# A written-out order for the first mixture, new pools for the second, and its first factors moved ahead

## The chip, the cores and the metric

The kernel runs on one core of a Trainium2 chip. Its time is the device time of one execution, in microseconds. A core has TensorE (PE in the profile; PEld are its weight loads), VectorE (DVE), ScalarE (ACT), GpSimd (POOL) and SyncE (SP, here only a queue for transfers). Each engine works through its own queue in order and waits there for results of the others.

## The reference, cut to what matters

```python
x = attention(q, k, v, centroids)       # 2 x 8 heads, 768 rows, width 64; (1536, 512) afterwards
h = x @ w_in                            # first mixture: (1536, 512) @ (512, 2048)
g = h * (1.0 / (1.0 + np.exp(-h)))
x = g @ w_out                           # (1536, 2048) @ (2048, 512)
P = sinkhorn(x @ w_gate)                # second mixture: eight experts, all of them for every row
for e in range(8):
    out += P[:, e:e+1] * (np.maximum(x @ w1[e], 0.0) @ w2[e])     # 512 -> 1024 -> 512
```

`w_in` and `w_out` come as 64-bit floats, the other inputs as 32-bit floats.

## The kernel before, in words

Products are made of a high and a low part: each operand is split into a rounded high part on ScalarE and the rest on VectorE or GpSimd, and three matmuls (high by high, high by low, low by high) stand for one.

The attention comes first and has an order written out by hand. The part of interest follows it.

*First mixture.* The 2048 hidden columns are cut into four slices. For each slice there are two passes of twelve tiles, so 8 passes and 96 tiles, numbered T = 0 to 95 here. A pass has three chunks of 512 rows, a chunk four tiles of 128 columns; a tile is twelve matmuls into one of eight PSUM banks (pool `mp`). In the first pass of a slice (L565 with `xh`, `xl`) a tile's result goes through a sigmoid on ScalarE (L582), a product on VectorE (L583, which is the last to read the bank), a high part on ScalarE (L584) and a low part on GpSimd (L585). In the second pass (L565 with `gh`, `gl`) a tile's result is added to `acc1`: a copy on ScalarE in the first slice (L598), a VectorE addition in the others (L600). These are called totals below.

The 64-bit weights are narrowed in steps: per pass one block n (n = 1 to 7 in these passes, block 0 during the attention), in four pieces of 128 x 512. A piece takes, on ScalarE, `wb` (L104), `w0` (L106) and the high part `wh` (L128); on VectorE `w1` (L107), `w2` (L109), `w3` (L110), `w4` (L112) and `wp1` (L114); on GpSimd `wp0` (L113) and the low part `wp2` (L129). Block n is narrowed while pass n - 1 runs. In this part the kernel leaves the order on each engine to the scheduler: the loop calls the four pieces of a block after the first four tiles of a pass, and the scheduler interleaves them.

*Second mixture.* Each of 16 slices (expert, half of its hidden width) has two layers of seven products (a scheme with seven block products in place of eight). A product of layer a is 24 matmuls (L815), one of layer b 36. The order of its instructions on four engines is written out by hand. Before a product, the weight's factor is split (`factor`: L713 on ScalarE, L638 on VectorE; tiles `wfh`, `wfl`), in slice 0 also x's factor (`x_factor`: L726, L638; `xfh`, `xfl`), some after sums of blocks of `acc1` (`x_sum`, L635). The blocks of `acc1` are halves of its rows by halves of its columns. In layer a the order of products is p = 1, 2, 6, 5, 7, 3, 4; products 1, 6, 7 and 4 add up in one set of three banks, and after product 1 ScalarE must copy this set (L852) before product 6 goes on with it. Between the last four stand the matmuls of the gate (L758, L765). The pools of this mixture are laid out one behind the other over the memory that the first mixture leaves, and a tile waits until whatever lies under it has been read for the last time.

Of the kernel before, what the change touches and what calls it, by code (L numbers as in the profile page):

```python
# [8 lines left out]
F32 = mybir.dt.float32  # L9
F32R = mybir.dt.float32r  # L10
# [3 lines left out]
ALU = mybir.AluOpType  # L14
# [24 lines left out]
def attention_moe_kernel(ctx, tc, kq, vp, cent, w_in, w_out, w_gate, w1, w2, out):  # L39
# [7 lines left out]
    def r(t):  # L47
        return t.bitcast(F32)
# [68 lines left out]
    def wsplit_steps(n, k, pool):  # L117

        tag = "ab"[n % 2]
        if k == 0:  # L120
            wts[n] = tuple(pools[n % 2].tile([P, 4, 512], F32R, name=f"w{c}{n}", tag=f"w{c}{tag}") for c in "hl")
        hi, lo = (t[piece_ix(n, k)] for t in wts[n])
        w = raws.pop((n, k))
        at, steps = (lambda c: w), {}

        if wide:
            at, steps = narrow_steps(w, pool, f"n{n}_{k}", nc.gpsimd if n == 0 else nc.vector)
        steps["wh"] = lambda: nc.scalar.copy(hi, at("a"))  # L128
        steps["wp2"] = lambda: nc.gpsimd.tensor_tensor(out=lo, in0=at("b"), in1=r(hi), op=ALU.subtract)  # L129
        return steps  # L130

    def wsplit(n, k, pool):

        for f in wsplit_steps(n, k, pool).values():
            f()
# [391 lines left out]
    def pool(stack, name, **kw):  # L527
        return stack.enter_context(tc.tile_pool(name=name, reuse_waits="tile", **kw))
# [11 lines left out]
    def next_load():  # L540
        if loads:
            n, k, m = loads.pop(0)
            wload(n, k, m, rp, 3)

    def splitter(n):

        if n >= nblk:
            return []

        def one(k):  # L550
            wsplit(n, k, tp)
            if k % 2 and (k == 3 or wide):
                next_load()

        return [lambda k=k: one(k) for k in range(4)]
# [12 lines left out]

    acc1 = accp.tile([P, KC, NTOK], F32, name="acc1", tag="acc")
    for s in range(F1 // FB):  # L570
        gh = gp.tile([P, NFT, NTOK], F32R, name=f"gh{s}", tag="gh")
        gl = gp.tile([P, NFT, NTOK], F32R, name=f"gl{s}", tag="gl")
        wb = splitter(2 * s + 1)
        wah, wal = wts.pop(2 * s)
        for c in range(NMC):
            cs = slice(c * MCH, (c + 1) * MCH)
            for ft in range(NFT):
                fs = slice(ft * P, (ft + 1) * P)
                ps = mp.tile([P, 512], F32, name=f"l1_{s}_{c}_{ft}", tag="m")
                mm3(ps, lambda k: wah[:, k, fs], lambda k: wal[:, k, fs], lambda k: xh[:, k, cs], lambda k: xl[:, k, cs])  # L580
                g = sp.tile([P, MCH], F32, name=f"g{s}_{c}_{ft}", tag="g")
                nc.scalar.activation(g, ps, AF.Sigmoid)  # L582
                nc.vector.tensor_tensor(out=g, in0=ps, in1=g, op=ALU.mult)  # L583
                nc.scalar.copy(gh[:, ft, cs], g)  # L584
                nc.gpsimd.tensor_tensor(out=gl[:, ft, cs], in0=g, in1=r(gh[:, ft, cs]), op=ALU.subtract)  # L585
                if wb:
                    wb.pop(0)()
        wa = splitter(2 * s + 2)
        wbh, wbl = wts.pop(2 * s + 1)
        for c in range(NMC):  # L590
            cs = slice(c * MCH, (c + 1) * MCH)
            for d in range(KC):
                ds_ = slice(d * P, (d + 1) * P)
                ps = mp.tile([P, 512], F32, name=f"l2_{s}_{c}_{d}", tag="m")
                mm3(ps, lambda k: wbh[:, k, ds_], lambda k: wbl[:, k, ds_], lambda k: gh[:, k, cs], lambda k: gl[:, k, cs])
                a = acc1[:, d, cs]
                if s == 0:
                    nc.scalar.copy(a, ps)  # L598
                else:
                    nc.vector.tensor_tensor(out=a, in0=ps, in1=a, op=ALU.add)  # L600
                if wa:
                    wa.pop(0)()
    mctx.close()


# [18 lines left out]
    wfp = pool(ctx, "wfp", bufs=5)  # L624
    wsp = pool(ctx, "wsp", bufs=2)
    hp = pool(ctx, "hp", bufs=1)
    ahp = pool(ctx, "ahp", bufs=5)
    sk = pool(ctx, "sk", bufs=1)
    ps3 = pool(ctx, "ps3", bufs=6, space=PSUM)
# [88 lines left out]
    def xblk(k, j):  # L718
        return acc1[:, 2 * k : 2 * k + 2, j * HT : (j + 1) * HT]
# [1 line left out]
    xf = {}  # L721

    def x_factor(p, x, e=vec):
        hi, lo = (xfp.tile([P, 2, HT], F32R, name=f"xf{c}{p}", tag=f"xf{c}{p}") for c in "hl")
        for k in range(2):
            act.copy(hi[:, k], x[:, k])  # L726
            lo_of(e, lo[:, k], x[:, k], hi[:, k])
        xf[p] = (hi, lo)

    def x_sum(out, in0, in1):  # L730
        for k in range(2):
            tt(vec, out[:, k], in0[:, k], in1[:, k], ALU.subtract)
# [228 lines left out]
    with tc.manual_schedule(engines={ENG.PE, ENG.DVE, ENG.Activation, ENG.Pool}):  # L961
        w_load(0)
        w_load(7)
        x_factor(1, xblk(0, 0))
        factor(0, vec)
        x_factor(2, xblk(1, 0))
        factor(1, vec)
        w_sums1(0, vec)
        psn = {}
        for n in range(14 * NS + 1):  # L970
            s, i = divmod(n, 14)
# [7 lines left out]
            if i == 0:  # L979
                if s == 0:  # L980
                    t2 = h_block(0, "21")
                    x_sum(xblk(0, 1), xblk(0, 1), xblk(0, 0))
                    x_sum(t2, xblk(1, 1), xblk(0, 1))
                    x_factor(6, t2)
                factor(n + 2, vec)
                w_sums2(n, vec)
                factor(n + 3, vec)
            if i == 1:
                if s == 0:
                    x_factor(5, xblk(0, 1))  # L990
                factor(n + 3, vec)
# [131 lines left out]
```

## Time and profile before

| | us |
|---|---|
| median of three runs | 1491.07 |
| the three runs | 1491.07, 1491.21, 1487.56 |
| the profiled execution | 1488.28 |
| its span, first to last instruction | 1486.4 |
| TensorE busy in it | 1460.4 |
| VectorE, ScalarE, GpSimd busy | 1063.7, 914.4, 489.5 |

The profile is of one execution. Busy time of an engine counts its instructions, overlaps once. A row of a timeline names an instruction's start, its length, its line, what it writes and reads, and in brackets how long the engine stood idle before it and what ended that. Buffer numbers are left out of names in the trace. Neighbouring instructions of an engine overlap a little at their ends, so that three of 0.69 in a row take less than 2.07.

### The profile page before, as it was taken

Reading aid. Unit: us, or ns where it says so; the run is one execution under the profiler, and the core shown is the slowest. Engines: PE = TensorE matmul, PEld = TensorE weight load, DVE = VectorE, ACT = ScalarE, POOL = GpSimd, SP = SyncE. Lnnn points to the kernel's source line nnn. Section 1 sums busy time; section 2 is a strip of 40 time slices with the busy share of each in tenths; the row PEclk is TensorE's granted clock in tenths of the full one; section 3 lists DMA queues with packets and bytes.
Section 4 is the critical chain, followed back from the end, with each engine's and each line's share of the span. In section 5 each row is a group of like instructions: output and inputs, shape, how many; then the busy total and the mean of one; then the engine's idle time right before and its main releaser. Section 6 shows DMA issues by size and latency. Waiting matters only on the chain.

```text
span 1486.4 us, 24728 instructions
## 1 busy us (share of the span) xinstructions
PE 1460.4 (98%) x9658; PEld 1296.7 (87%) x9659; DVE 1063.7 (72%) x1617; ACT 914.4 (62%) x1754; POOL 489.5 (33%) x441
## 2 busy tenths in 40 slices
PE   8999999999999999999999999999999999999997
PEld 5777787878888789998999999999999999999997
DVE  6788777776672698856768568577685685776857
ACT  6677765553533376656667586576675865766754
POOL 6688855655654001145121121120211211202111
PEclk9999999999999999999999999999999999999999
DMA  6665622221101027497795694874956958749565
GB/s 200 170 179 148 166 77 86 86 85 57 57 2 57 0 69 166 71 234 164 122 198 87 120 161 87 165 118 93 201 77 130 153 92 167 118 92 200 79 124 107
DMA packets 132230, 177.03 MB, mean 119 GB/s; under 512 B 5904, under 2 KB 101392, under 8 KB 132112
## 3 DMA queue, kind: packets, MB, share of 16 engines
q0 software_dynamic: 82976, 86.91, 38.2%
q1 hardware_dynamic: 48992, 88.50, 19.3%
q8 instruction: 76, 1.25, 0.3%
q14 instruction: 42, 0.34, 0.1%
q10 hardware_dynamic: 144, 0.03, 0.0%
HBM read 64.54 MB, written 88.87 MB: 103 GB/s over the span
## 4 chain that ended last, share of the span: by engine, by line
PE 91%; DVE 4%; DMA 2%; POOL 1%; issue 1%; ACT 1%; DVEq 0%; ACTq 0%; POOLq 0%
PE b L815 31%; PE a L815 31%; PE l L565 14%; PE av L345 4%; PE t L323 4%; PE s L285 3%; PE s L286 2%; DMA out_dram<-acc 1%; PE gl L758 0%; DVE acc L903 0%; PE sim L189 0%; DVE g L583 0%; POOL gl L585 0%; POOL wl L129 0%; DVE n_1b L114 0%
## 5 line engine op out<-in xcount | busy, mean ns | idle before, releaser
L928 POOL DMA_DIRECT2D out_dram<-acc x101 | 146.6, 1696 | 756.3 <-ACT acc L922 438.3
L815 PE MATMUL b<-wfh,ah 128*128 128x256 f32 x1344 | 381.1, 284 | 1.5 <-ACT acc L922 1.1
L815 PE MATMUL b<-wfl,ah 128*128 128x256 f32 x1344 | 380.4, 283 | 0.0
L815 PE MATMUL b<-wfh,al 128*128 128x256 f32 x1344 | 380.3, 283 | 0.0
L815 PE MATMUL a<-xfh,wfh 128*128 128x512 f32 (+1 forms) x896 | 303.6, 339 | 4.4 <-ACT acc L922 2.0
L815 PE MATMUL a<-xfl,wfh 128*128 128x512 f32 (+1 forms) x896 | 303.2, 338 | 0.0
L815 PE MATMUL a<-xfh,wfl 128*128 128x512 f32 (+1 forms) x896 | 302.0, 337 | 0.9 <-DVE wfl L638 0.9
L815 PEld LDWEIGHTS b<-wfh,ah 128*128 128x128 f32 x1344 | 257.9, 192 | 2.9 <-ACT acc L922 1.6
L815 PEld LDWEIGHTS b<-wfl,ah 128*128 128x128 f32 x1344 | 257.9, 192 | 0.7
L815 PEld LDWEIGHTS b<-wfh,al 128*128 128x128 f32 x1344 | 257.9, 192 | 0.0
L922 ACT ACTIVATE acc<-b,Pg 128x256 f32<-128x256 f32 x484 | 188.7, 496 | 29.9 <-issue 18.7
L865 ACT CAST ah<-h 128x768 fp32r<-128x768 f32 x192 | 158.8, 861 | 66.0 <-DVE h L947 26.0
L815 PEld LDWEIGHTS a<-xfh,wfh 128*128 128x128 f32 x896 | 170.7, 190 | 24.1 <-ACT acc L922 2.5
L638 DVE TENSOR_TENSOR al<-h,ah 128x768 fp32r<-128x768 f32 x192 | 177.2, 957 | 19.5 <-ACT ah L865 18.9
L815 PEld LDWEIGHTS a<-xfh,wfl 128*128 128x128 f32 x896 | 170.2, 190 | 20.0 <-DVE wfl L638 1.4
L815 PEld LDWEIGHTS a<-xfl,wfh 128*128 128x128 f32 x896 | 170.7, 191 | 16.9
L638 DVE TENSOR_TENSOR wfl<-w0r,wfh 128x512 fp32r<-128x512 f32 x96 | 64.8, 689 | 81.4 <-ACT wfh L713 79.4
L635 DVE TENSOR_TENSOR h<-a,h 128x512 f32<-128x512 f32 x144 | 94.3, 686 | 27.0 <-PE a L815 26.1
L852 ACT COPY h<-a 128x512 f32<-128x512 f32 x144 | 81.0, 591 | 46.1 <-PE a L815 46.0
L304 ACT ACTIVATE p<-s,m 128x768 f32<-128x768 f32 x96 | 86.7, 905 | 30.8 <-DVE m L295 28.2
L295 DVE TENSOR_REDUCE m<-s 128x1 f32<-128x768 f32 x96 | 89.9, 952 | 15.9 <-PE s L286 15.0
L314 POOL TENSOR_SCALAR p<-p,rec 128x768 f32<-128x768 f32 x96 | 85.8, 907 | 43.9 <-DVE rec L309 31.0
(204 smaller groups left out, 2612.9 us busy)
## 6 DMA issues: line engine op xcount, KB each, us to landing
out_dram<-acc POOLq DMA_DIRECT2D x101, 768.0 KB, 10.0
w0r<-in_w_dram SPq DMA_DIRECT2D x16, 1024.0 KB, 8.3
w1r<-in_w_dram SPq DMA_DIRECT2D x16, 1024.0 KB, 6.9
qk<-qk SPq DMA_DIRECT2D x45, 192.0 KB, 3.6
raw<-in_w_out_dram SPq DMA_DIRECT2D x8, 1024.0 KB, 4.9
raw<-in_kq_dram SPq DMA_DIRECT2D x16, 384.0 KB, 4.5
raw<-in_w_in_dram SPq DMA_DIRECT2D x6, 1024.0 KB, 5.2
out_dram<-acc SPq DMA_DIRECT2D x8, 768.0 KB, 4.0
```

Of the source, the lines that this page charges most:

```text
L295: nc.vector.tensor_reduce(out=m, in_=tiles[i]["s"][:, :S], axis=AX.X, op=ALU.max, negate=True)
L304: nc.scalar.activation(t["p"], t.pop("s")[:, :S], AF.Exp, bias=t.pop("m"), accum_out=chunks[c]["sum"][:, j, 0:1])
L314: nc.gpsimd.tensor_scalar(out=p, in0=p, scalar1=chunks[c]["rec"][:, j : j + 1], scalar2=1.0, op0=ALU.mult, op1=ALU.mult)
L323: nc.tensor.transpose(ps[:, b * P : (b + 1) * P], tiles[2 * c + j]["p"][:, kt * P : (kt + 1) * P], ident)
L565: nc.tensor.matmul(ps, lhsT=s(k), rhs=m(k), start=n == 0, stop=n == 11)
L635: e.tensor_tensor(out=out, in0=in0, in1=in1, op=op)
L638: e.tensor_tensor(out=lo, in0=x, in1=r(hi), op=ALU.subtract)
L815: nc.tensor.matmul(ps[bank][:, cols], lhsT=lf(i, k), rhs=rt(j, k), start=first and bank not in opened, stop=k == 1 and q == 2, skip_group_ ...
L852: act.copy(bank(t, u), ps[u])
L865: act.copy(hi, x)
L922: act.mul(t[:, 2 * u + m], z[:, m], g)
L928: gps.dma_start(out=out_block(i, j), in_=t, accum_op=ALU.add)
```

## The change

The loops of the first mixture give way to a table: for each tile T it says which steps of which tiles and weight pieces follow (with a place within the slot), and all four engines take exactly this order. Two pieces of a block are narrowed side by side, each step for both. A weight load is issued as soon as the last of its buffer's readers has been put in the order. The twelve tiles of the last pass keep no written order: there the scheduler may mix the totals with what the second mixture begins with. The second mixture's pool for x factors loses two of seven (for products 3 and 4) to a new pool `xlp` behind `hp`, so that `wfp`, `wsp` and part of `hp` come to lie lower. Its first factors are called earlier. The work itself, and TensorE's order, are the same. The core of the diff (the old loops, which stand above, are cut, and of the table one line is left):

```diff
     def wsplit_steps(n, k, pool):
-        if k == 0:
-            wts[n] = tuple(pools[n % 2].tile([P, 4, 512], F32R, name=f"w{c}{n}", tag=f"w{c}{tag}") for c in "hl")
-        hi, lo = (t[piece_ix(n, k)] for t in wts[n])
+        def part(i):
+            if n not in wts:
+                wts[n] = tuple(pools[n % 2].tile([P, 4, 512], F32R, name=f"w{c}{n}", tag=f"w{c}{tag}") for c in "hl")
+            return wts[n][i][piece_ix(n, k)]
...
+    def sig(T):
+        gs[T] = sp.tile([P, MCH], F32, name=f"g{T}", tag="g")
+        nc.scalar.activation(gs[T], banks[T], AF.Sigmoid)
+
+    def mult(T):
+        nc.vector.tensor_tensor(out=gs[T], in0=banks.pop(T), in1=gs[T], op=ALU.mult)
...
+    def total(T):
+        s, _, cs, f = where(T)
+        a, ps = acc1[:, f, cs], banks.pop(T)
+        if s == 0:
+            nc.scalar.copy(a, ps)
+        else:
+            nc.vector.tensor_tensor(out=a, in0=ps, in1=a, op=ALU.add)
...
+    LAYER1 = ((sig, 2, 20), (mult, 3, 3), (g_hi, 4, 2), (g_lo, 5, 10))
+    BEGIN = {1: (-1, -1, 4, 4), 0: (-2, -2, 3, 3)}
+    STEPS = {
...
+        0: dict(w0=(0, 6), wb=(2, 1), w1=(0, 16), w2=(2, 7), w3=(2, 11), w4=(2, 13), wh=(3, 18), wp0=(4, 17), wp1=(5, 22), wp2=(6, 19)),
+    }
...
+    for T in range((2 * NS1 - 1) * HALF):
+        if T // HALF % 2 == 0:
+            for f, late, place in LAYER1:
+                put(T + late, place, f, T)
+        else:
+            put(T + 1, 4, total, T)
+    for n in range(1, nblk):
+        for k in range(4):
+            begin = HALF * (n - 1) + BEGIN[n % 2][k] - (3 if n % 2 and n > 1 else 0)
+            for w, (late, place) in STEPS[n % 2].items():
+                put(begin + late, place, narrow_step, n, k, w)
+
+    with tc.manual_schedule(engines={ENG.PE, ENG.DVE, ENG.Activation, ENG.Pool}):
+        for T in range(min(slots), max(slots) + 1):
+            for _, _, f, args in sorted(slots.get(T, []), key=lambda x: x[0]):
+                f(*args)
+            if 0 <= T < (2 * NS1 - 1) * HALF:
+                tile1(T)
+    for T in range((2 * NS1 - 1) * HALF, 2 * NS1 * HALF):
+        tile1(T)
+        total(T)
     mctx.close()
...
+    xlp = pool(ctx, "xlp", bufs=1)
...
     def x_factor(p, x, e=vec):
-        hi, lo = (xfp.tile([P, 2, HT], F32R, name=f"xf{c}{p}", tag=f"xf{c}{p}") for c in "hl")
+        hi, lo = ((xlp if p in (3, 4) else xfp).tile([P, 2, HT], F32R, name=f"xf{c}{p}", tag=f"xf{c}{p}") for c in "hl")
...
         w_load(0)
         w_load(7)
+        factor(0, vec)
+        factor(1, vec)
         x_factor(1, xblk(0, 0))
-        factor(0, vec)
+        w_sums1(0, vec)
+        w_sums2(0, vec)
         x_factor(2, xblk(1, 0))
-        factor(1, vec)
-        w_sums1(0, vec)
+        factor(2, vec)
+        factor(3, vec)
+        factor(4, vec)
+        x_sum(xblk(0, 1), xblk(0, 1), xblk(0, 0))
+        x_factor(5, xblk(0, 1))
```

On ScalarE, in the second pass, this is the order before, from the first total of slice 0 on (`l2_0_0_1` is slice 0, chunk 0, column tile 1 of a second pass; `n3_1u` is block 3, piece 1, buffer `u`):

```order
L598 COPY acc1_3138<-l2_0_0_0_3415 128x512
L104 ACTIVATE n2_3b_3514<-raw2_1_3205 128x512
L128 CAST wh2_3429<-n2_3a_3520 128x4x128
L104 ACTIVATE n3_0b_3663<-raw3_0_3269 128x512
L106 ACTIVATE n3_0u_3665<-raw3_0_3269 128x512
L598 COPY acc1_3138<-l2_0_0_1_3444 128x512
L104 ACTIVATE n3_1b_3694<-raw3_0_3269 128x512
L106 ACTIVATE n3_1u_3696<-raw3_0_3269 128x512
L598 COPY acc1_3138<-l2_0_0_2_3473 128x512
L106 ACTIVATE n3_2u_3729<-raw3_1_3471 128x512
L106 ACTIVATE n3_3u_3760<-raw3_1_3471 128x512
L598 COPY acc1_3138<-l2_0_0_3_3500 128x512
```

Between the first total and the fourth stand eight narrowing steps, six of them of block 3.

And the order after, from the same total on (`l12` is tile 12, the first of the second pass; `g11` the sigmoid of tile 11):

```order
L602 COPY acc1_3138<-l12_3426 128x512
L130 CAST wh2_3443<-n2_0a_3416 128x4x128
L130 CAST wh2_3443<-n2_1a_3418 128x4x128
L582 ACTIVATE g11_3447<-l11_3394 128x512
L591 CAST gh0_3228<-g10_3424 128x512
L602 COPY acc1_3138<-l13_3449 128x512
L591 CAST gh0_3228<-g11_3447 128x512
L602 COPY acc1_3138<-l14_3468 128x512
L106 ACTIVATE n2_2u_3483<-raw2_1_3172 128x512
L106 ACTIVATE n2_3u_3485<-raw2_1_3172 128x512
L602 COPY acc1_3138<-l15_3492 128x512
L104 ACTIVATE n2_2b_3522<-raw2_1_3172 128x512
```

The last sigmoid and high parts of the first pass have moved behind the first totals, and the steps of block 3 have gone to later tiles.

On VectorE, at the end of the first mixture, this is the order before, from the total of tile 91 on (`w0r0`: the first weight block of the second mixture; `ws0`: a sum of its parts; the last row is the first x sum):

```order
L600 TENSOR_TENSOR acc1_3138<-l2_3_1_3_5013,acc1_3138 128x512
L600 TENSOR_TENSOR acc1_3138<-l2_3_2_0_5027,acc1_3138 128x512
L600 TENSOR_TENSOR acc1_3138<-l2_3_2_1_5041,acc1_3138 128x512
L600 TENSOR_TENSOR acc1_3138<-l2_3_2_2_5055,acc1_3138 128x512
L600 TENSOR_TENSOR acc1_3138<-l2_3_2_3_5069,acc1_3138 128x512
L638 TENSOR_TENSOR wfl0_5142<-w0r0_5131,wfh0_5141 128x512
L638 TENSOR_TENSOR xfl2_5146<-acc1_3138,xfh2_5145 128x768 x2
L638 TENSOR_TENSOR wfl1_5152<-w0r0_5131,wfh1_5151 128x512
L635 TENSOR_TENSOR w0r0_5131<-w0r0_5131 128x2x256
L635 TENSOR_TENSOR ws0_5155<-w0r0_5131 128x512
L635 TENSOR_TENSOR acc1_3138<-acc1_3138 128x768 x2
```

The four totals behind the first row come without anything between them, and the splits and sums follow the last of them.

And the order after, from just behind the total of tile 91 on (`l92` to `l95` are the last tiles' results):

```order
L688 TENSOR_TENSOR xfl2_5161<-acc1_3138,xfh2_5160 128x768 x2
L688 TENSOR_TENSOR wfl2_5167<-ws0_5155,wfh2_5166 128x512
L604 TENSOR_TENSOR acc1_3138<-l92_5030,acc1_3138 128x512
L688 TENSOR_TENSOR wfl3_5171<-w0r0_5137,wfh3_5170 128x512
L688 TENSOR_TENSOR wfl4_5175<-w0r0_5137,wfh4_5174 128x512
L685 TENSOR_TENSOR acc1_3138<-acc1_3138 128x768
L604 TENSOR_TENSOR acc1_3138<-l93_5044,acc1_3138 128x512
L685 TENSOR_TENSOR acc1_3138<-acc1_3138 128x768
L688 TENSOR_TENSOR xfl5_5181<-acc1_3138,xfh5_5180 128x768
L604 TENSOR_TENSOR acc1_3138<-l94_5058,acc1_3138 128x512
L688 TENSOR_TENSOR xfl5_5181<-acc1_3138,xfh5_5180 128x768
L604 TENSOR_TENSOR acc1_3138<-l95_5072,acc1_3138 128x512
```

The splits for products 2 and 5 and the weight factors 2 to 4 now stand between the totals of tiles 91 and 95.

## Rows read from the trace of the kernel before

**Rows 1.** The page's first part: busy time, share of the span, instructions
```profile
span 1486.4 us, 24728 instructions
...
PE 1460.4 (98%) x9658; PEld 1296.7 (87%) x9659; DVE 1063.7 (72%) x1617; ACT 914.4 (62%) x1754; POOL 489.5 (33%) x441
```

**Rows 2.** Timeline of PE, first mixture: start us, us, what, [idle before <-releaser]
```profile
236.05 0.50 PE L565 MATMUL l<-xh,wh 128*128 128x512 f32 x1
...
302.62 0.50 PE L565 MATMUL l<-gh,wh 128*128 128x512 f32 x1 [2.91 <-ACT acc L598]
...
303.31 0.63 PE L565 MATMUL l<-gh,wl 128*128 128x512 f32 x1
...
307.06 0.39 PE L565 MATMUL l<-xh,wh 128*128 128x512 f32 x1
```

**Rows 3.** Busy time in two stretches: length, PE, PEld, DVE, ACT, POOL, PEclk, DMA
```profile
236.00:256.00 20.00, 20.00 (x89) 16.53 (x89) 16.10 (x21) 11.65 (x21) 11.26 (x9) 1.00 0.20 58
296.00:316.00 20.00, 16.60 (x65) 13.12 (x65) 14.42 (x18) 11.68 (x23) 10.45 (x7) 0.91 0.31 105
```

**Rows 4.** Timeline of ACT around the wait of PE
```profile
301.43 0.68 ACT L106 ACTIVATE n_3u<-raw 128x512 f32<-128x512 f32 x1 [2.27 <-POOL n_1b L113]
302.01 3.98 ACT L598 COPY acc<-l 128x512 f32<-128x512 f32 x8
```

**Rows 5.** Timeline of PE at the start of the second mixture
```profile
502.90 0.39 PE L815 MATMUL a<-xfh,wfh 128*128 128x512 f32 x1
...
504.44 0.50 PE L815 MATMUL a<-xfh,wfl 128*128 128x512 f32 x1 [0.93 <-DVE wfl L638]
...
513.97 0.50 PE L815 MATMUL a<-xfh,wfh 128*128 128x512 f32 x1 [1.34 <-ACT h L852]
...
519.49 0.47 PE L815 MATMUL a<-xfh,wfh 128*128 128x512 f32 x1 [1.02 <-DVE h L635]
```

**Rows 6.** Timeline of ACT at the start of the second mixture
```profile
510.70 1.70 ACT L726 CAST xfh<-h 128x768 fp32r<-128x768 f32 x2 [6.92 <-DVE h L635]
...
513.35 1.55 ACT L852 COPY h<-a 128x512 f32<-128x512 f32 x3
```

**Rows 7.** Timeline of DVE at the start of the second mixture
```profile
503.10 0.69 DVE L600 TENSOR_TENSOR acc<-l,acc 128x512 f32<-128x512 f32 x1 [2.03 <-PE l L565]
...
504.31 1.82 DVE L638 TENSOR_TENSOR xfl<-acc,xfh 128x768 fp32r<-128x768 f32 x2
...
509.71 1.82 DVE L635 TENSOR_TENSOR h<-acc 128x768 f32<-128x768 f32 x2
```

**Rows 8.** The chain that ended last, in order of time: start us, us, what
```profile
544.66 4.31 PE b L815 x36
...
637.58 29.29 PE a L815 x168
```

**Rows 9.** Six narrowing steps, 236 to 503: count, shortest/median/longest ns, starts
```profile
L109 DVE TENSOR_SCALAR n_0u<-n_0u x7: 414/1392/1519, 241.3 to 423.5; 128x512 uint32<-128x512 uint32 x7
...
L110 DVE SCALAR_TENSOR_TENSOR n_3a<-raw,n_3u x7: 679/1779/1784, 258.8 to 440.1; 128x512 uint32<-128x512 uint32 x7
...
L112 DVE TENSOR_SCALAR n_2u<-n_2a x7: 414/911/1403, 254.5 to 441.8; 128x512 uint32<-128x512 uint32 x7
...
L113 POOL TENSOR_TENSOR n_2b<-n_2b,n_2u x7: 1337/1740/1752, 255.5 to 442.3; 128x512 f32<-128x512 f32 x7
...
L114 DVE TENSOR_TENSOR n_0b<-n_0a,n_0b x7: 680/1767/1785, 246.1 to 427.9; 128x512 f32<-128x512 f32 x7
...
L129 POOL TENSOR_TENSOR wl<-n_0b,wh x7: 1293/1742/1802, 248.0 to 438.3; 128x512 fp32r<-128x512 f32 x7
```

**Rows 10.** Timeline of PE at its later wait
```profile
705.26 0.50 PE L815 MATMUL a<-xfh,wfh 128*128 128x512 f32 x1 [2.02 <-ACT acc L922]
```

**Rows 11.** Loads: engine, count, KB each, us from issue to landing
```profile
wgr<-in_w_gate_dram SPq DMA_DIRECT2D x1, 16.0 KB, 7.0
...
w0r<-in_w_dram SPq DMA_DIRECT2D x1, 1024.0 KB, 5.1
```

More of the change, by code (lines that the diff above doesn't have):

```diff
@@ L127, in wsplit_steps @@
             at, steps = narrow_steps(w, pool, f"n{n}_{k}", nc.gpsimd if n == 0 else nc.vector)
-        steps["wh"] = lambda: nc.scalar.copy(hi, at("a"))
-        steps["wp2"] = lambda: nc.gpsimd.tensor_tensor(out=lo, in0=at("b"), in1=r(hi), op=ALU.subtract)
+        steps["wh"] = lambda: nc.scalar.copy(part(0), at("a"))
+        steps["wp2"] = lambda: nc.gpsimd.tensor_tensor(out=part(1), in0=at("b"), in1=r(part(0)), op=ALU.subtract)
         return steps
@@ L543, in next_load @@
             wload(n, k, m, rp, 3)
[L545 to L555, printed above, removed]
     for _ in range(3):
@@ L569, in attention_moe_kernel @@
     acc1 = accp.tile([P, KC, NTOK], F32, name="acc1", tag="acc")
[L570 to L602, printed above, removed]
@@ new lines, in attention_moe_kernel, with where, tile1 @@
+    NS1, HALF = F1 // FB, NMC * NFT
+    banks, gs, ghl, parts, unread = {}, {}, {}, {}, {}
+    def where(T):
+        s, x = divmod(T, 2 * HALF)
+        layer, x = divmod(x, HALF)
+        c, f = divmod(x, NFT)
+        return s, layer, slice(c * MCH, (c + 1) * MCH), f
+    def tile1(T):
+        s, layer, cs, f = where(T)
+        if layer:
+            mv_hi, mv_lo = ghl[s]
+        else:
+            mv_hi, mv_lo = xh, xl
+        whi, wlo = wts[2 * s + layer]
+        fs = slice(f * P, (f + 1) * P)
+        ps = banks[T] = mp.tile([P, 512], F32, name=f"l{T}", tag="m")
+        mm3(ps, lambda k: whi[:, k, fs], lambda k: wlo[:, k, fs], lambda k: mv_hi[:, k, cs], lambda k: mv_lo[:, k, cs])
@@ new lines, in sig, with g_hi, g_lo @@
+    def sig(T):
[3 more added lines that the diff above has]
+        nc.vector.tensor_tensor(out=gs[T], in0=banks.pop(T), in1=gs[T], op=ALU.mult)
+    def g_hi(T):
+        s, _, cs, f = where(T)
+        if s not in ghl:
+            ghl[s] = tuple(gp.tile([P, NFT, NTOK], F32R, name=f"g{w}{s}", tag=f"g{w}") for w in "hl")
+        nc.scalar.copy(ghl[s][0][:, f, cs], gs[T])
+    def g_lo(T):
+        s, _, cs, f = where(T)
+        hi, lo = (t[:, f, cs] for t in ghl[s])
+        nc.gpsimd.tensor_tensor(out=lo, in0=gs.pop(T), in1=r(hi), op=ALU.subtract)
@@ new lines, in total, with narrow_step @@
+    def total(T):
+        s, _, cs, f = where(T)
+        a, ps = acc1[:, f, cs], banks.pop(T)
[3 more added lines that the diff above has]
+            nc.vector.tensor_tensor(out=a, in0=ps, in1=a, op=ALU.add)
+    def narrow_step(n, k, w):
+        if (n, k) not in parts:
+            parts[n, k] = wsplit_steps(n, k, tp)
+        f = parts[n, k].pop(w, None)
+        if f:
+            f()
+        m = n, k // 2 if wide else 0
+        unread.setdefault(m, {(k, w) for k in range(2 * m[1], 2 * m[1] + 2) for w in ("wb", "w3")} if wide else {(k, w) for k in range(4) for w in ("wh", "wp2")})
+        if (k, w) in unread[m]:
+            unread[m].remove((k, w))
+            if not unread[m]:
+                next_load()
@@ new lines, in attention_moe_kernel, with put @@
+    LAYER1 = ((sig, 2, 20), (mult, 3, 3), (g_hi, 4, 2), (g_lo, 5, 10))
+    BEGIN = {1: (-1, -1, 4, 4), 0: (-2, -2, 3, 3)}
+    STEPS = {
+        1: dict(w0=(0, 9), wb=(2, 8), w1=(1, 5), w2=(1, 14), w3=(1, 21), w4=(1, 23), wh=(4, 15), wp0=(3, 24), wp1=(4, 12), wp2=(5, 0)),
+        0: dict(w0=(0, 6), wb=(2, 1), w1=(0, 16), w2=(2, 7), w3=(2, 11), w4=(2, 13), wh=(3, 18), wp0=(4, 17), wp1=(5, 22), wp2=(6, 19)),
+    }
+    slots = {}
+    def put(T, place, f, *args):
+        slots.setdefault(T, []).append((place, len(slots), f, args))
@@ new lines, in attention_moe_kernel @@
+    for T in range((2 * NS1 - 1) * HALF):
+        if T // HALF % 2 == 0:
+            for f, late, place in LAYER1:
+                put(T + late, place, f, T)
+        else:
+            put(T + 1, 4, total, T)
[4 more added lines that the diff above has]
+                put(begin + late, place, narrow_step, n, k, w)
+    ENG = mybir.EngineType
@@ L981, in attention_moe_kernel @@
                     t2 = h_block(0, "21")
-                    x_sum(xblk(0, 1), xblk(0, 1), xblk(0, 0))
                     x_sum(t2, xblk(1, 1), xblk(0, 1))
                     x_factor(6, t2)
-                factor(n + 2, vec)
-                w_sums2(n, vec)
-                factor(n + 3, vec)
+                else:
+                    factor(n + 2, vec)
+                    w_sums2(n, vec)
+                    factor(n + 3, vec)
             if i == 1:
-                if s == 0:
-                    x_factor(5, xblk(0, 1))
-                factor(n + 3, vec)
+                if s:
+                    factor(n + 3, vec)
                 factor(n + 4, vec)
```

## Prediction

> **What bounds the kernel now.** I read the page's head first: TensorE is busy 98% of a span of 1486.4 us [rows 1], so only time in which TensorE waits or runs slowly can be won, and the total of its matmuls cannot shrink, since the change touches no product. Next comes the order of time on TensorE. The first mixture is 96 tiles of twelve matmuls. Its first matmul starts at 236.05, tile 24's at 307.06, the second mixture's at 502.90 [rows 2, 5]. The last 72 tiles take 195.84 us, 2.72 each; at that pace the first 24 would take 65.28, but they take 71.01. So 5.7 us are lost there and nothing later in that mixture. The reader is to see where: a wait of 2.91 us in front of tile 23, ended by ScalarE's copy of a result, and then matmuls of 0.63 us, so that tile 23 takes 4.44 us (302.62 to 307.06) and not 2.72: 1.7 us more [rows 2]. The stretch around it has a granted clock of 0.91, a mix of the full 2.4 GHz and the lower 1.2 GHz [rows 3].
>
> What was ScalarE doing? Its rows show a wait of 2.27 us for a GpSimd step of the narrowing, and then eight result copies in one run from 302.01 [rows 4]. The finished tiles were there; ScalarE's queue held narrowing steps of the weights in front of their copies, and TensorE ran out of its eight PSUM banks.
>
> The second place is the start of the second mixture. A product of its first layer is 24 matmuls; seven take 29.29 us between 637.58 and 666.87, so one takes 4.18 [rows 8]. The first three should take 12.55 us from 502.90; the fourth starts at 519.49, after 16.59 [rows 5]. So 4.0 us are lost. TensorE waited for a low factor (to 504.44), for ScalarE's copies of the first product (to 513.97) and for VectorE's additions (to 519.49). The causes stand in ScalarE's and VectorE's rows: the first factors are split after the last total at 503.10, factor 2 of x at 504.31, the sum for factor 6 at 509.71, and ScalarE waits 6.92 us for that sum while the copies of the first product stand behind it [rows 6, 7].
>
> **First mixture in a fixed order.** No instruction is added. In the second pass ScalarE's order becomes one copy per tile, with no more than two narrowing steps between one copy and the next, where eight stood between the first and the fourth copy. I follow it with TensorE's pace: tile T ends at 236.05 + 2.72 x (T+1). Copy 14 is due at 276.9. Behind it on ScalarE are two first steps of block 2, 0.68 each as in row 301.43 [rows 4]: 277.6 and 278.3. VectorE then does two steps of one kind (pieces 2 and 3, at the longest 1.52 each from 277.6, taken like L109), to 280.6; two additions (pieces 0 and 1, 1.78 each), to 284.2; three steps for each of pieces 2 and 3 (1.52, 1.78, 1.40), to 293.6. GpSimd's two multiplications (1.75) begin beside the last of these, at 292.2, and end at 295.7; VectorE's addition (1.78) and GpSimd's subtraction (1.80) follow, to 299.3 [rows 9]. By the shortest of the same rows the end is near 287. Tile 24 needs the weights at 236.05 + 24 x 2.72 = 301.3. So even the long sum leaves 2.0 us, and I take no wait. ScalarE's two steps that wait for GpSimd's low parts of pieces 0 and 1 (at the longest 286.0) stand ahead of copies 16 and 17, due at 282.3 and 285.0; these come late by some 5 us, and their bank is needed again only eight tiles on, 19 us after a tile's end.
>
> In the first pass the load is VectorE's: before its eleventh product (tile 10) the order has 28 narrowing instructions and 10 products. From 236 to 256, 21 instructions of the same kinds took 16.10 us, 0.77 each [rows 3]; 38 make 29.1 us. They can begin at about 237.4, an estimate: the first matmul's start plus two of ScalarE's steps of 0.68. That ends at 266.5, and with an allowance of 7 us of idle time at 273.5. Tile 18 needs that bank at 285.0. At worst every narrowing instruction takes 1.6 us, near the longest rows, and a product 0.7: 44.8 + 7.0, so 289.2, 4.2 too late. I take the mean, since it is of the same mix beside the same GpSimd work. So the whole 5.7 us come back; the lower bound of this part is that 4.2 us are lost to a new wait and 1.7 to the clock after it, 5.9, and nothing is won. A small load moves: the gate's weights come behind one more weight load on SP's queue and take 7.0 us to land [rows 11]; that weight load waits for six steps that VectorE ends near 241 (from 237.4, by the shortest rows), so ScalarE can cast them near 249, and what stands behind the cast waits for tile 5's end at 252.4: nothing. More than 5.7 cannot be won, since the other 72 tiles are already at pace.
>
> The rows show VectorE's narrowing steps at 0.41 or at 1.52 for one and the same shape [rows 9]. The Trainium skill (SBUF — State Buffer, Who interferes with whom) says that VectorE and GpSimd share a port pair, and that an instruction which needs it is held until the other engine's has ended; the spread agrees with it. Read strictly it speaks against this change, which sets the steps of two pieces next to one another beside GpSimd's; the price by it is that of the first rival below.
>
> **The second mixture's start.** The new pool order puts the weight factors over memory that the weight steps of the first mixture leave early, where before the second one waited for the last matmul. Fifteen VectorE instructions and their ScalarE casts move ahead of the end. The place to check is VectorE from the total of tile 91, at 503.10 - 4 x 2.72 = 492.22: four totals and three low factors of weights at 0.69 and six half-width x steps at 0.91 (1.82 for two) [rows 7] make 4.83 + 5.46 = 10.29, to 502.5; the last total is due at 503.10, so it is not late. The load of its first weights can start when tile 83 has ended, at 502.90 - 12 x 2.72 = 470.3, and lands 5.1 us later [rows 11], at 475.4; VectorE comes to them behind the total of tile 85, due at 475.9.
>
> After it the sum for factor 6 takes 1.82, to 505.7, ScalarE casts the halves beside it, and the low part takes one cast and 1.82, to 508.4. Product 3 (p 6) starts at 502.90 + 2 x 4.18 = 511.26: 2.9 to spare. ScalarE is free at about 507.4, product 1 has ended at 507.1, so its copies (1.55) are there by 509.0: 2.3 to spare [rows 6]. The fourth product needs the second's banks: VectorE's three additions, 0.69 each, run from 511.3 to 513.4; it starts at 502.90 + 12.55 = 515.45: 2.0 to spare. So the 4.0 us come back whole. From 519.49 to the second layer at 544.66 [rows 5, 8] are 25.17 us, four products (16.7) and the gate's matmuls between them; VectorE has less to do there than before, so they move as they are. What is late next is the known wait at 705.26 on outputs [rows 10], which hangs on products that all move alike.
>
> Sum: 5.7 + 4.0 = 9.7. The profiled execution took 1488.28 (1.9 us around its span), so 1478.6. The three runs shown are 1487.56, 1491.07 and 1491.21; the middle of all four is 1489.7. I set the forecast against that: 1480.
>
> **Rivals.** (1) The port holds VectorE in the first pass: the wait of 4.2 plus 1.7 comes in place of the old one, and only the start of the second mixture is won: 1489.7 - 4.0 + 0.2 = 1485.9. For it: the long rows; against it: the mean of 0.77 over the same mix. (2) The start is won only in part: factor 6 is late because totals and splits crowd VectorE, and the second and third wait stay; the wait for the low factor goes, 1.1 us (504.44 against 503.36, the next matmul's turn). 1489.7 - 5.7 - 1.1 = 1482.9. For it: VectorE has no gap from 492.2 on; against it: 2.0 us or more to spare at each step. (3) The 4.0 us are given back at 705.26: if the transfers there follow a pace of their own, 1484.0. Against it: they carry products of the second layer, which come earlier by as much. (4) Slower: the narrowing of blocks 2, 4 and 6 in the second, fourth and sixth pass is one chain over three in-order queues, and if it takes 4 us more than the 2.0 to spare beyond the long sum, TensorE waits 4 at tiles 24, 48 and 72 and pays 1.7 for the clock each time: 17.1 against 9.7 won, 1497. It decides from a wait of 1.5 us at each, where 3 x 3.2 eat the gain. For it: the queue's steps now wait in pairs; against it: the long sum already has the longest row of every step.
>
> **Chances.** Forecast 0.70, with a range of its own from 1476 to 1484 (the runs shown lie 3.7 apart); rival 1 0.10, rival 2 0.08, rival 3 0.05, rival 4 0.07. About 0.3%, 4.5 us, is what a measurement of this kernel can tell: rivals 2 and 3 are faster beyond it, rival 1 stands at its edge and counts mostly as no change, as does a small part of the forecast. That makes 0.80 faster, 0.13 within, 0.07 slower. The range that leaves out rival 4 and the tails runs from 1475 to 1487.
>
> **What would show it.** In the profile after, the first matmul of the second mixture should stand 261.1 us behind the first of the first mixture, with the granted clock at 1.00 throughout, ScalarE's copies one per tile, and no wait on them. The fourth product should start 12.6 us after the first, and the second layer 37.7 after it. A wait in front of tile 18 to 20 shows rival 1; one in front of tiles 24, 48 or 72 rival 4; a third product later than 8.4 us after the first shows rival 2; a longer wait than 2.0 where 705.26 is now shows rival 3. I am wrong if the tiles of the first mixture come out slower than 2.72 without any wait.

## The result, and the profile after

The changed kernel took 1475.41 us in the median of four runs (1474.18 to 1479.09), the one before 1491.14 beside it: a ratio of 0.9901, with a 95% interval of 0.9876 to 0.9927. Forecast were 1480 us and a range of 1475 to 1487. In a second comparison, told below, the same changed kernel came out at 0.9936 (0.9917 to 0.9955), 9.5 us on 1487.1; the forecast sum was 9.7. Both medians moved between the comparisons (1475.41 to 1478.2, and 1491.14 to 1487.1), and the two intervals overlap. A wait that comes and goes from run to run, which the middle part of this document finds, is worth up to 5 us; that it alone makes the gap is not shown.

The profiled execution took 1475.02 us. The first part of its page, beside [rows 1], shows the same TensorE work in a span that is 13.2 us shorter:

```profile
span 1473.2 us, 24744 instructions
...
PE 1457.1 (99%) x9659; PEld 1295.3 (88%) x9659; DVE 1039.4 (71%) x1617; ACT 912.7 (62%) x1754; POOL 482.6 (33%) x441
```

The chain that ended last, in order of time (start us, us, what), answers to [rows 2, 5, 8, 10]:

```profile
238.29 261.34 PE l L555 x1152
499.63 16.72 PE a L865 x96
...
537.08 4.32 PE b L865 x36
...
672.55 17.42 PE b L865 x143
689.97 29.58 PE a L865 x168
719.55 30.23 PE b L865 x252
```

The 1152 matmuls of the first mixture stand in one piece, with no wait in them, and so do the first four products of the second mixture. At the place of [rows 10] nothing stands either: slice 2 and the first layer of slice 3 run on, and the longest gap in them is 0.20 us. In the stretch that answers to the second of [rows 3] TensorE is busy throughout, at full clock (length, PE, PEld, DVE, ACT, POOL, PEclk, DMA):

```profile
298.00:318.00 20.00, 20.00 (x90) 16.57 (x89) 11.54 (x16) 11.34 (x20) 12.20 (x10) 1.00 0.32 105
```

ScalarE's rows there show one copy per tile, each as soon as its tile has ended, and between them two narrowing steps that wait for GpSimd, which make the next copy 1.4 us late and no more (compare [rows 4]):

```profile
273.91 0.59 ACT L602 COPY acc<-l 128x512 f32<-128x512 f32 x1 [3.74 <-PE l L555]
...
282.07 0.59 ACT L602 COPY acc<-l 128x512 f32<-128x512 f32 x1 [1.01 <-PE l L555]
283.90 0.68 ACT L104 ACTIVATE n_2b<-raw 128x512 f32<-128x512 uint32 x1 [1.24 <-POOL wl L131]
285.34 0.68 ACT L104 ACTIVATE n_3b<-raw 128x512 f32<-128x512 uint32 x1 [0.76 <-POOL wl L131]
285.92 0.58 ACT L602 COPY acc<-l 128x512 f32<-128x512 f32 x1
```

At the start of the second mixture ScalarE (ahead of it VectorE's sum) has product 1 copied out by 504.4, where the third product is due at 499.47 + 8.36 = 507.8; before, those copies came at 513.35 [rows 6]:

```profile
501.26 1.70 ACT L776 CAST xfh<-h 128x768 fp32r<-128x768 f32 x2 [4.03 <-DVE h L685]
502.87 1.57 ACT L902 COPY h<-a 128x512 f32<-128x512 f32 x3
```

Where the 13.2 us of the spans are, by place (from the two chains; the second mixture's first matmul from PE's timelines):

| stretch | before | after | gain |
|---|---|---|---|
| up to the first matmul of the first mixture | 236.1 | 238.3 | -2.2 |
| from there to the second mixture's first matmul | 266.8 | 261.2 | 5.6 |
| from there to its second layer | 41.8 | 37.6 | 4.2 |
| from layer b of slice 0 to layer b of slice 3 | 187.5 | 182.5 | 5.0 |
| the rest | 754.2 | 753.7 | 0.6 |

The second and third lines are the two terms of the forecast, 5.7 and 4.0. The first and the fourth were not in it.

### The profile page after: what moved, and what is told of

It reads as the page before. It is cut to its first block, busy times and chain, and to the rows that moved or that the text cites. A ratio compares the mean times of both kernels' runs of the same rounds, so it can differ in the third digit from the quotient of the medians.

```text
span 1473.2 us, 24744 instructions
## 1 busy us (share of the span) xinstructions
PE 1457.1 (99%) x9659; PEld 1295.3 (88%) x9659; DVE 1039.4 (71%) x1617; ACT 912.7 (62%) x1754; POOL 482.6 (33%) x441
## 4 chain that ended last, share of the span: by engine, by line
PE 98%; DVE 1%; DMA 0%; ACT 0%; issue 0%; POOL 0%; DVEq 0%; ACTq 0%; POOLq 0%
PE b L865 32%; PE a L865 32%; PE l L555 18%; PE av L347 4%; PE t L325 4%; PE s L287 3%; PE s L288 2%; PE gl L808 0%; DVE acc L953 0%; PE sim L191 0%; DMA cr<-in_cent_dram 0%; PE oht L261 0%; PE simt L202 0%; ACT qk L505 0%; DVE oh L497 0%
## 5 line engine op out<-in xcount | busy, mean ns | idle before, releaser
L978 POOL DMA_DIRECT2D out_dram<-acc x101 | 146.5, 1678 | 750.6 <-ACT acc L972 437.1
```

The lines of the kernel that those rows point to most:

```text
L978: gps.dma_start(out=out_block(i, j), in_=t, accum_op=ALU.add)
```

## The experiments

All are timed against the kernel before. "us faster" is the measured ratio applied to the median of the kernel before; that ratio is not quite the quotient of the two medians shown, so the differences of the medians come out up to 1.6 us apart from it. The first four take the change apart.

**The written order alone** (the first mixture's half of the diff above, nothing else).

> The kernel before with the first mixture's written order alone (pools and first factors of the second mixture as before). My theory (the wait before tile 23 and the lower clock behind it are the whole loss of that mixture, and the order alone takes them away): the second mixture's first matmul stands 261.2 us behind the first mixture's (266.85 before), the fourth product 16.6 behind that one, as before; the whole 5.6 us faster than before, some 1485 against 1490.5. Rival (the order pays only together with the new start, since the last pass and the first factors share VectorE): under 3 us faster. On the unforecast 4.9 us between the second layers of slices 0 and 3: if that wait comes from the phase in which transfers and GpSimd's rescaling fall beside VectorE, it may be there or not whatever the edit, between 182.6 and 187.5 us from layer b of slice 0 to that of slice 3; if the change of the start takes it away, it is there in full, 187.5.

Measured: 1482.67 against 1489.25, ratio 0.9962 (0.9949 to 0.9974), 5.7 us faster. From first matmul to first matmul 261.2 us, the second layer 41.8 behind, the three waits of [rows 5] all there:

```profile
499.94 0.50 PE L864 MATMUL a<-xfh,wfl 128*128 128x512 f32 x1 [0.93 <-DVE wfl L687]
509.47 0.50 PE L864 MATMUL a<-xfh,wfh 128*128 128x512 f32 x1 [1.32 <-ACT h L901]
514.99 0.47 PE L864 MATMUL a<-xfh,wfh 128*128 128x512 f32 x1 [1.05 <-DVE h L684]
```

The order stands by itself and is worth the first term whole. It sets several things at once (which steps stand ahead of a copy, two pieces side by side, when a block begins); which of them would be enough was not tried.

**The new start alone** (the pool `xlp` and the earlier calls).

> The kernel before with the second mixture's new pools and early factors alone (first mixture in the scheduler's order). My theory: the wait before tile 23 stays, 266.9 us from first matmul to first matmul; the second layer comes 37.5 behind the second mixture's first matmul (41.8 before), so 4.3 us faster. Rival (the start needs the written order too): the fourth product later than 13.5 behind the first, under 2 us faster. If the change of the start takes the wait at the outputs of slice 2 away as well: 182.6 from layer b of slice 0 to that of slice 3, and 9 us faster in all.

Measured: 1482.92, ratio 0.9968 (0.9953 to 0.9982), 4.8 us faster. 266.9 and 37.6 us in the two stretches, as the theory had it; 185.5 in the stretch of the unforecast gain.

**The two halves of the start, each alone.** The pool:

```diff
+    xlp = pool(ctx, "xlp", bufs=1)
...
-        hi, lo = (xfp.tile([P, 2, HT], F32R, name=f"xf{c}{p}", tag=f"xf{c}{p}") for c in "hl")
+        hi, lo = ((xlp if p in (3, 4) else xfp).tile([P, 2, HT], F32R, name=f"xf{c}{p}", tag=f"xf{c}{p}") for c in "hl")
```

> The kernel before with the new pool xlp alone, factors called in the old order. My theory (memory that is free early lets the scheduler put the splits between the last totals, but ScalarE's copies of product 1 still stand behind a cast that waits for VectorE's weight sums): the low-factor wait goes, the third product's wait shrinks from 1.34 to about 1.5 us at most, in all 2 to 3 us faster than before. Rival (pools are what matters, the calls nothing): 4 us faster, fourth product 12.6 behind the first.

and the earlier calls over the old pools:

> The kernel before with the first factors called earlier, old pools. My theory (under the old pools the tile of the second weight factor lies over memory that the last matmul of the first mixture reads, so all that is called behind it is late, and factors 2 to 4 and the split for product 5 now stand ahead of the sum and split for product 6): the third product comes some 8 us later than before, near 19 us behind the first, and the whole is 3 to 8 us slower than before. Rival (the calls are what matters): 3 to 4 us faster.

Measured: the pool alone 1482.75, ratio 0.9964 (0.9950 to 0.9977), 5.4 us faster; the calls alone 1494.61, ratio 1.0040 (1.0024 to 1.0056), 6 us slower. So the rival was right about the pool: by its chain the whole gain is there without the calls,

```profile
505.36 16.72 PE a L816 x96
...
542.81 4.31 PE b L816 x36
```

37.6 us from the first matmul (505.20) to the second layer. With the memory free early, the splits go between the last totals even in the old order of calls, and ScalarE reaches product 1's copies at 509.64, with the third product due at 513.6. My 1.5 us of remaining wait came from setting VectorE's weight sums ahead of casts that don't need them: the two weight casts ahead of the copies ran at 508.61 and 509.12 without a wait, and those sums followed at 510.21. The calls alone show the other side. ScalarE stands in front of a weight cast until the last matmul of the first mixture has read what lies under its tile, and product 1's copies come behind the casts for products 5 and 6, which wait for VectorE's sums (rows of ACT, then of PE):

```profile
503.31 0.62 ACT L713 CAST wfh<-w0r 128x512 fp32r<-128x512 f32 x1 [26.86 <-PE l L565]
...
517.59 1.70 ACT L726 CAST xfh<-h 128x768 fp32r<-128x768 f32 x2 [1.90 <-DVE h L635]
519.20 1.56 ACT L852 COPY h<-a 128x512 f32<-128x512 f32 x3
```

```profile
519.83 0.50 PE L815 MATMUL a<-xfh,wfh 128*128 128x512 f32 x1 [3.61 <-ACT h L852]
```

The size was as expected (3 to 8 us); the third product came 15.1 us behind the first and not 19. The first matmul itself waited too, 1.50 us for ScalarE's cast behind that weight cast, which is why the table below has 268.3 us in front of it.

**The copies on another engine** (kernel before): is it ScalarE, or the order?

```diff
                 if s == 0:
-                    nc.scalar.copy(a, ps)
+                    nc.vector.tensor_copy(a, ps)
```

> The kernel before, in the scheduler's order, with one edit: the totals of the first slice are copied by VectorE (as those of the other slices already are) and not by ScalarE. Theory (TensorE waits before tile 23 only because those copies stand on ScalarE behind narrowing steps that wait for GpSimd; on VectorE no more than four narrowing steps stand between two totals, and none of them waits long): from the first matmul of the first mixture to that of the second 261.2 to 262 us (266.8 before), some 5 us faster than before, with no written order at all. Rival (the written order itself is what keeps the pace, a copy engine alone is not enough): a wait of 1.5 us or more stays or comes in another place of the first mixture, 264 us or more.

Measured: 1487.72 against 1488.08, ratio 0.9995 (0.9981 to 1.0010); 265.9 us, so only 0.9 us come back. My theory fell and the rival stands. The wait has changed engines; PE's rows, then VectorE's:

```profile
296.75 0.50 PE L565 MATMUL l<-gh,wh 128*128 128x512 f32 x1 [0.79 <-DVE acc L598]
...
300.66 0.50 PE L565 MATMUL l<-gh,wh 128*128 128x512 f32 x1 [0.90 <-DVE acc L598]
...
305.49 0.50 PE L565 MATMUL l<-gh,wh 128*128 128x512 f32 x1 [1.80 <-DVE acc L598]
```

```profile
302.46 1.77 DVE L114 TENSOR_TENSOR n_0b<-n_0a,n_0b 128x512 f32<-128x512 f32 x1 [1.19 <-POOL n_0b L113]
304.16 0.68 DVE L114 TENSOR_TENSOR n_1b<-n_1a,n_1b 128x512 f32<-128x512 f32 x1
304.76 0.68 DVE L598 COPY acc<-l 128x512 f32<-128x512 f32 x1
```

A total stands behind a narrowing step that waits for GpSimd, here as there. In the kernel before, ScalarE waited four times for GpSimd between its first copy (286.64) and its fourth (302.01), 9.05 us in all; these are the first three, and the fourth is in [rows 4]:

```profile
291.46 0.67 ACT L104 ACTIVATE n_0b<-raw 128x512 f32<-128x512 uint32 x1 [3.16 <-POOL wl L129]
...
294.95 0.67 ACT L104 ACTIVATE n_1b<-raw 128x512 f32<-128x512 uint32 x1 [1.78 <-POOL wl L129]
...
298.48 0.67 ACT L106 ACTIVATE n_2u<-raw 128x512 f32<-128x512 f32 x1 [1.84 <-POOL n_0b L113]
```

In the changed kernel two such waits are left ahead of a copy, 1.24 and 0.76 us (283.90 and 285.34 above), and the copy is 1.4 us late. So what the written order wins is not a lighter ScalarE; it is that fewer of these waits add up in front of the totals.

**The unforecast 5 us.** In slice 2 the outputs of the first expert, written unscaled, are read back (four blocks), rescaled by GpSimd in 24 instructions, and written again; only then are the four output buffers free for layer b. First the changed kernel once more, without an edit:

> The changed kernel once more, unchanged. Theory A (the 4.9 us between the second layers of slices 0 and 3 that came without being forecast are a matter of when the read-back blocks land, which differs from run to run; in four kernels with parts of the change that stretch took 182.66, 184.06, 184.33 and 185.54 us): the runs spread over 5 us, the median lies near 1477, and the profile may show anything from 182 to 187.5 us. Theory B (the change takes that wait away): 182.5 us again, and the runs lie within 2 us of 1475.

Measured: 1478.2 (1474.59 to 1481.15), ratio 0.9936; and its profile has the whole wait of [rows 10], 187.6 us:

```profile
685.66 0.39 PE L865 MATMUL b<-wfh,ah 128*128 128x256 f32 x1 [0.96 <-ACT acc L972]
...
696.61 0.72 PE L865 MATMUL a<-xfh,wfh 128*128 128x512 f32 x1 [2.03 <-ACT acc L972]
697.12 0.63 PE L865 MATMUL a<-xfl,wfh 128*128 128x512 f32 x1
```

So the change did not take that wait away; the first profile of it happened to be without. What differs is seen on GpSimd. The two profiles of the same changed kernel, first the earlier one, then this:

```profile
648.69 23.27 POOL L1076 TENSOR_SCALAR acc<-acc,Pg 128x256 f32<-128x256 f32 x24 [16.00 <-DMA acc<-out_dram]
```

```profile
649.09 25.66 POOL L1076 TENSOR_SCALAR acc<-acc,Pg 128x256 f32<-128x256 f32 x24 [17.54 <-DMA acc<-out_dram]
```

Against layer b of slice 0 (537.08 and 535.94) GpSimd could begin on the first block at +111.6 and at +113.2: 1.5 us apart, and it was through at +134.9 and +138.8, 3.9 apart. One of its instructions takes (count, shortest/median/longest ns):

```profile
L1076 POOL TENSOR_SCALAR acc<-acc,Pg x24: 470/478/1967, 648.7 to 670.0; 128x256 f32<-128x256 f32 x24
```

Fifteen of the 24 take 0.47 to 0.49 us, one 0.93 and eight 1.96 to 1.97. The long ones lie beside a run of VectorE instructions of 1.0 us each, that begins at 653.74. It is broken once, by three of 0.68 that read a PSUM bank (`a`), and beside these GpSimd is back at 0.48:

```profile
653.74 2.10 DVE L997 SCALAR_TENSOR_TENSOR h<-h,h 128x768 f32<-128x768 f32 x2
655.77 1.87 DVE L685 TENSOR_TENSOR h<-a,h 128x512 f32<-128x512 f32 x3
...
661.92 2.01 DVE L1003 SCALAR_TENSOR_TENSOR h<-h,h 128x768 f32<-128x768 f32 x2
663.86 2.02 DVE L685 TENSOR_TENSOR h<-h,h 128x768 f32<-128x768 f32 x2
665.80 2.02 DVE L688 TENSOR_TENSOR al<-h,ah 128x768 fp32r<-128x768 f32 x2
```

What GpSimd gets done before that run costs it 0.5 us an instruction, what falls into it up to 2 us; so a late start counts more than once. That VectorE's run is what holds GpSimd is read from these rows; no run here takes it away. The Trainium skill (SBUF — State Buffer, Who interferes with whom) has it that a VectorE instruction with two inputs in SBUF contends with a GpSimd instruction that reads SBUF, and that ScalarE never waits on anyone. The rows above agree with the first half. For the second, the next experiment's six ScalarE instructions took 0.50 to 0.51 us each beside the same run.

**One of the four blocks on ScalarE**, behind its copies of product 4, where it stood idle 2.25 us; in the changed kernel and in the kernel before:

```diff
-            if i in (3, 4, 5, 6) and s == 2:
-                t, c = again[i - 3]
+            if i in (3, 4, 5, 7) and s == 2:
+                t, c = again[min(i - 3, 3)]
                 for m in range(6):
+                    if i == 7:
+                        act.mul(t[:, m], t[:, m], Pg[:, 6 * c[0] + m, 0:1])
+                        continue
                     gps.tensor_scalar(out=t[:, m], in0=t[:, m], scalar1=Pg[:, 6 * c[0] + m, 0:1], scalar2=1.0, op0=ALU.mult, op1=ALU.mult)
```

> The changed kernel, but the fourth read-back block of slice 2 (six instructions) is rescaled on ScalarE, behind its copies of product 4 of layer a, where it stood idle 2.25 us, and not on GpSimd. Theory A (GpSimd's rescaling, held by VectorE's long instructions beside it, makes the rewriting and so the output buffers late): the rescaling on GpSimd ends some 6 us earlier relative to layer b, the fourth rewriting is issued near +126 and not +134.8 us behind layer b of slice 0, the stretch from layer b of slice 0 to that of slice 3 takes 182.0 or less, the same in every run, so the spread of the runs shrinks and the median falls by 1 to 3 us against the changed kernel, to some 1473.5. Rival (the transfers' own pace makes the buffers late): no change, 182.5 to 187.5. Other rival (ScalarE's six steps hold its high parts for layer b): a new wait of up to 2 us in slice 2.

> The kernel before with the same single edit: the fourth read-back block of slice 2 rescaled on ScalarE. Theory A: the stretch from layer b of slice 0 to that of slice 3 falls from 187.5 to 182.0, the waits of 1.07 and 2.02 us and the lower clock behind them go, and the median falls by 3 to 5 us. Rival (the transfers' own pace): no change, the waits stay.

Measured: changed kernel with it 1474.52 (1472.54 to 1475.75), ratio to before 0.9911 (0.9893 to 0.9930), where the changed kernel beside it had 0.9936, an interval that overlaps with this one; kernel before with it 1484.01 (1482.97 to 1485.46) against 1487.1 (1484.11 to 1491.46), ratio 0.9977 (0.9966 to 0.9987), 3.4 us faster. The stretch takes 181.7 and 181.9 us, although in the second GpSimd began latest of all profiles, at +113.7. The runs of the kernel before spread over 7.4 us, with the edit over 2.5. In the changed kernel GpSimd is through with its 18 by 662.4, and the last two rewritings are issued at +125.2 and +126.1 (rows of POOL, ACT and SP):

```profile
649.27 13.11 POOL L1079 TENSOR_SCALAR acc<-acc,Pg 128x256 f32<-128x256 f32 x18 [16.43 <-DMA acc<-out_dram]
```

```profile
660.85 2.50 ACT L1077 ACTIVATE acc<-acc,Pg 128x256 f32<-128x256 f32 x6
```

```profile
662.40 1.35 SPq L1080 DMA_DIRECT2D out_dram<-acc  x2
```

The rewritings are not all that a late GpSimd holds up. GpSimd also issues the transfers of layer b's own outputs (L978), and they stand behind the rescaling in its queue. The chain of the profile with the whole wait (the changed kernel once more) runs through these:

```profile
673.41 1.34 POOL acc L1076 x2
674.75 1.65 POOL out_dram L978 x2
676.40 19.21 DMA out_dram<-acc
...
696.61 26.93 PE a L865 x144
```

The edit makes both earlier, and how much either is worth alone was not tried.

**GpSimd made late** (changed kernel): three multiplications by 1.0 ahead of the first block.

```diff
                 t, c = again[i - 3]
+                if i == 3:
+                    for m in range(3):
+                        gps.tensor_scalar(out=t[:, m], in0=t[:, m], scalar1=1.0, scalar2=1.0, op0=ALU.mult, op1=ALU.mult)
```

> The changed kernel with three more instructions of GpSimd (a multiplication by 1.0, 128x256 each, 0.47 us alone) ahead of the rescaling of the first read-back block of slice 2. Theory A: the rescaling ends some 3 us later, the wait for the outputs comes back, 186 to 188 us from layer b of slice 0 to that of slice 3, 3 to 5 us slower than the changed kernel. Rival (transfers alone): at most 0.5 us slower.

Measured: 1479.98 (1479.03 to 1482.81), ratio 0.9952 (0.9935 to 0.9969); 187.6 us. GpSimd began as early as in the first profile, at +111.6, and 1.15 us more of its work brought the whole wait back in the profile:

```profile
649.28 1.15 POOL L1077 TENSOR_SCALAR acc<-acc 128x256 f32<-128x256 f32 x3 [15.99 <-DMA acc<-out_dram]
650.41 25.68 POOL L1079 TENSOR_SCALAR acc<-acc,Pg 128x256 f32<-128x256 f32 x24
```

Its median is 1.8 us above the changed kernel's beside it, less than the 3 to 5 expected, and the two intervals overlap; the likely reason, seen in one profile of that kernel but not in its other runs, is that it has the wait in some of its own. By the stretch, Theory A holds: when GpSimd is through with its blocks decides. Why it can begin up to 2 us earlier or later from run to run stays open. Of the 1.5 us between the two profiles of the changed kernel 0.4 are a later issue of the first read-back, and 1.1 a longer time from there to GpSimd's start (12.8 and 13.9 us).

**The change without its earlier calls**, with the fourth block on ScalarE:

> The changed kernel with the fourth block rescaled on ScalarE, but with the first factors of the second mixture called in the old order: the change without its last part. Theory (the new pools alone win the start; the calls add nothing): 37.5 us from the second mixture's first matmul to its second layer, as with them, and a median within 1 us of the version that has them, 1474.5. Rival (under the first mixture's new order the calls matter): the second layer later than 38.5 us behind the first matmul, 1 to 4 us slower.

Measured: 1473.81 (1472.52 to 1474.47), ratio 0.9912 (0.9897 to 0.9927), 37.6 us to the second layer. The calls add nothing once the pool is there. This version and the one with them are the fastest that ran.

All profiles together (us; the rescaling's start counts from layer b of slice 0, the last column is the stretch from there to layer b of slice 3):

| kernel | first mixture | start of second | rescaling starts | takes | stretch |
|---|---|---|---|---|---|
| before | 266.8 | 41.8 | 113.0 | 25.7 | 187.5 |
| written order alone | 261.2 | 41.8 | 112.3 | 24.5 | 184.1 |
| new start alone | 266.9 | 37.6 | 112.1 | 25.3 | 185.5 |
| pool alone | 266.8 | 37.6 | 111.8 | 23.3 | 182.7 |
| calls alone | 268.3 | 46.0 | 112.2 | 24.5 | 184.3 |
| copies on VectorE | 265.9 | 41.8 | 112.4 | 24.5 | 184.2 |
| changed | 261.2 | 37.6 | 111.6 | 23.3 | 182.5 |
| changed, again | 261.2 | 37.6 | 113.2 | 25.7 | 187.6 |
| changed, GpSimd late | 261.2 | 37.6 | 112.7 | 25.7 | 187.6 |
| before, a block on ScalarE | 266.8 | 41.8 | 113.7 | 18.3 (18) | 181.9 |
| changed, a block on ScalarE | 261.2 | 37.6 | 112.0 | 13.1 (18) | 181.7 |
| the same without the earlier calls | 261.2 | 37.6 | 112.0 | 13.2 (18) | 181.7 |

In order of the rescaling's end (start and length added up) the stretch grows through all twelve, whatever the edit, but for steps of 0.2 us or less: 181.7 to 181.9 us with an end at +132 or before, 182.5 to 182.7 near +135, 184.1 to 184.3 near +136.8, 185.5 at +137.4, and 187.5 to 187.6 from +138.4 on.

## Why the prediction was right, point by point

*The 5.7 us of the first mixture.* Right: 5.6, and the order alone gives them. The granted clock is at 1.00 in every 20 us from 238 to 498, and no tile waits. The margins were wider than reckoned. Block 2's last low part ended at 293.4, with tile 24 due at 303.6 in that profile: 10 us to spare, against 2.0 by the long sum, because most VectorE steps were short there. VectorE's eleventh product ended at 273.7, against a deadline of 287.2 (18 x 2.72 behind 238.29): the mean was the right choice, and rival 1 did not come. Copy 16 came 1.4 us late, not 5. Rival 4's waits at tiles 24, 48 and 72 are absent.

*Its reason.* I said that ScalarE's queue held narrowing steps in front of the copies. That is what the rows show, but the copy engine is not the point: on VectorE the same wait arose. The place that has to be named is the GpSimd result that a narrowing step waits for, ahead of a total, and how many such waits stand there.

*The 4.0 us of the start.* Right in size: 4.2, and rival 2 did not come. The reason was half right. Pools and calls were reckoned as one part; the pool is all of it, and the calls over the old pools would have cost 6 us. In the prediction the new pool order was called what lets the factors move; that their calls need not move was not seen.

*The wait at 705.26.* "Hangs on products that all move alike" was the weak step. It does not hang on the products alone; it hangs on when GpSimd is through with the read-back blocks beside VectorE's work, and is worth 0 to 5 us in a profile. The 4.0 us were not given back there: the stretch was never longer than before by more than 0.1 us. So rival 3 is out by the stretch, though the sign named for it, a wait longer than 2.0, is no good: with the new start alone that wait was 2.29 us, and the stretch was 2.0 shorter than before. That the first profile showed the place without a wait was chance. The median of four runs was 4.6 us better than forecast and lies 0.4 inside the range; that it lies inside is in part luck, since the ratio of that comparison is worth 14.8 us where the sum said 9.7. In the second comparison the ratio gives 9.5. The two terms at their full value are borne out by the parts; what lies beyond them differs from run to run.

*Not foreseen and not caused:* the first mixture starts anywhere from 236.1 to 238.9 us in these profiles, without a relation to the edits that they show: the changed kernel alone gave 238.3 and 237.2.

## What to carry to other kernels

When several engines in order share a pipeline, look for the instruction that releases a PSUM bank and at what stands in front of it; steps that wait for a third engine must not add up there, and here moving the release to another engine moved the wait along. Memory that is free early can be worth more than code that is called early: here the first won its 4.2 us alone, and the second without the first cost 6. And a wait can be there in one profile of a kernel and gone in the next, so one profile does not show that an edit took it away; such a wait belongs in the range and not in the sum.

## What was not expected of the hardware

A rescaling of 24 equal GpSimd instructions (0.47 us each when undisturbed, so 11.3) took 23.3 to 25.7 us beside VectorE, and a start 1.5 us later made its end 3.9 us later. The same multiplication on ScalarE took 0.51 us each beside the same VectorE work. A wait of 2.91 us left TensorE with matmuls of 0.63 us behind it [rows 2] and a granted clock of 0.83, a mix of its two levels of 2.4 and 1.2 GHz, in the ten us from 298; with waits of 0.79, 0.90 and 1.80 us at the same place, in the kernel with the copies on VectorE, the granted clock stayed at 1.00:

```profile
298.00:308.00 10.00, 7.09 (x25) 5.41 (x24) 5.32 (x9) 6.21 (x12) 2.04 (x3) 0.83 0.32 105
```

```profile
298.00:308.00 10.00, 7.31 (x31) 5.37 (x30) 8.81 (x18) 1.55 (x3) 2.60 (x2) 1.00 0.32 106
```

The first row is of the kernel before, the second of that one.
